# Attention, soft experts and MLP on one core: other spacing of converted weights, and products of zeros at the handover

## The chip, the cores and the metric

One Trainium2 chip, one of its cores. The metric is the device time of one execution in microseconds. The core's engines are TensorE (PE; its weight loads are PEld), VectorE (DVE), ScalarE (ACT), GpSimd (POOL) and SyncE (SP), which here only issues DMAs. Each engine executes its own queue in order.

## The reference

Three layers follow each other. Inputs are random; w_in, w_out, s and b of the last layer are 64-bit floats.

```python
def _attn_ref(q, k, v, cap):                       # (4, 12, 448, 64)
    scores = np.matmul(q, k.transpose(0, 1, 3, 2)) / np.sqrt(64)
    scores = cap * np.tanh(scores / cap)
    attn = np.exp(scores - np.max(scores, axis=-1, keepdims=True))
    attn = attn / (np.sum(attn, axis=-1, keepdims=True) + 1e-09)
    return np.matmul(attn, v)
def _moe_ref(x, phi, w1, w2):                      # x (1792, 768), 8 experts of 4 slots
    logits = x @ phi
    d = softmax(logits, axis=0); c = softmax(logits, axis=1)
    slot_input = (d.T @ x).reshape(8, 4, 768)
    for e in range(8):
        slot_out[e] = np.maximum(slot_input[e] @ w1[e], 0.0) @ w2[e]
    return c @ slot_out.reshape(32, 768)
def _moe2_ref(x, w_in, w_out, s, b):               # w_in (768, 2048), w_out (2048, 768)
    r = np.maximum(x @ w_in, 0.0)
    return (s * (r * r) + b) @ w_out
```

## The kernel before

The work has three stages on one core.

**Attention** (to about 257 us). For each of 24 pairs of heads, n, TensorE makes scores (`emit_qk`, L498, and `emit_qkl`, L515), ScalarE takes tanh and exp (L521, L535), VectorE and GpSimd add the exponentials (`emit_es`, `emit_esl`, L543, L549), and TensorE multiplies by v (`emit_av`, L556, `emit_avl`, L564). Copies out of PSUM (`copy`, L421 on ScalarE, L423 on VectorE) go to either engine. After every six pairs a softmax over tokens is carried on (`emit_smax`, `emit_sexp`, `emit_softt`, `emit_pn` at L716, `emit_slot` at L723, `emit_acc`).

Between this work the first weights of the MLP are turned from 64-bit floats to 32-bit ones. One block i is 128 rows of words: even i are blocks of w_in, odd i of w_out. A conversion is a load of 768 KB (`cv_load`, L208), two VectorE passes (`conv_a`, L221 and L224), one ScalarE pass (`conv_f`, L231), a sum on VectorE or GpSimd (`conv_m`, L234) and a store of 384 KB to a scratch tensor in DRAM (`cv_store`, L342), from which the MLP reloads it (`load_w`, L1117). 2*XS = 20 blocks of 32 are converted so; the others are loaded and converted during the MLP. Expert weights are loaded too (`load_next`, L364 for w1, L370 for w2): 14 blocks in rings that are open from the start, and six more of w2 in a ring that takes over the conversion's buffers (`cv_end`), so they come after the last store.

The order on each engine comes from `ListSchedule`: every operation has engines with planned costs, needs, a priority, buffers that it takes and frees, a latency that is added to its end (`lat`) and an earliest planned time (`after`). A candidate with a third number (the handicaps `HACT`, `DES`, `DESL`) is chosen as if it ended that much later. CV0 and CVP give a conversion's priority, CVA and CVT its load's earliest planned time, WA that of expert loads. Planned times set the order alone; at run time each engine waits for what it needs.

**Experts** (267 to 342 us). For each expert e, `emit_w1` (L1008) multiplies the slots by three blocks of w1, `emit_w1_t` transposes and takes the maximum with 0, `emit_w2` (L1029) multiplies by four blocks of w2 into `so`. The products of e+1 with w1 are issued ahead of those of e with w2. As blocks are used up their rings are reloaded. Further blocks lie in the room that attention's pools leave: two of w1, three of w2 (pools `px`) and four of w2 in `woe`.

**MLP** (to the end). `emit_sot` (L1278) transposes `so`. Since the first product of the MLP is linear in the slots, w_in is applied to these: for each of 16 blocks f, `emit_ma` (L1160) multiplies block and slots, `emit_ms` (L1168, ScalarE) copies the sum, `emit_mb` (L1173) repeats it over partitions, `emit_mc` (L1181, ScalarE) casts it, `emit_ml` (L1184, VectorE) keeps its rounding error. Then for each step x (512 tokens, one f; 16 values of f, then the next tokens): `emit_h` (L1191), the activation in four ScalarE passes (L1208, L1215 and twice L1221) to gh, its rounding error gl on VectorE (`emit_gl`, L1236), and `emit_y`, for each 128 tokens six products (L1254, L1255) with the high and low part of w_out. Those parts are made by `emit_hi` (a cast, L1146 on ScalarE, L1148 on VectorE, which it may use for f < FD = 3) and `emit_lo` (L1151, GpSimd). A second `ListSchedule` orders this stage. It plans `sot` at a time given by `after`, and everything that needs the slots behind that.

Of the kernel before, what the change touches and what calls it, by code (L numbers as in the profile page):

```python
# [10 lines left out]
F32 = mybir.dt.float32  # L11
# [91 lines left out]
def kernel(  # L103
# [87 lines left out]
    NE1 = KDM * FC  # L191
    XS = 10 if wide else 0
    scr_p = ctx.enter_context(tc.tile_pool(name="scr", bufs=1, space=bass.MemoryType.DRAM))
# [99 lines left out]
    def run(safe):  # L293
        W1N, W2N = (4, (4,)) if safe else (10, (4, 6))
        NV, NEB, NES, NXU, NXQ, NQK = 2, 5, 2, 4, 3, 2
        PX, PA, DES, DESL, HACT = -0.32, 2.0, 1.0, 0.5, 0.5
        CV0, CVP, CVA, CVT, WA = 9.33, 2.0, 20.19, 9.5, 30.39
        LATE = 0.6
# [593 lines left out]
        for bb in range(B):  # L892
            g = NQUAD * (bb + 1) - 1
            pr = 4 * g + 4 + PSO
            prev = [("ssum", bb - 1)] if bb else []
            op(("soft", bb), [(PE, 0.38)], emit_soft, [("lgr", g)], pr, [("tp", ("soft", bb))], [("lw", g)])
            op(("smax", bb), [(DVE, 0.66)], emit_smax, [("soft", bb)] + prev, pr, [("nm", bb)])
            op(
                ("sexp", bb), [(ACT, 0.8)], emit_sexp, [("smax", bb)], pr, [("pt", bb), ("al", bb)],
                [("tp", ("soft", bb))],  # L900
            )
            op(("ssum", bb), [(DVE, 0.2)], emit_ssum, [("sexp", bb)] + [("pn", bb)] * (bb == B - 1), pr + 1, [], [("nm", bb), ("al", bb)])
            op(("softt", bb), [(PE, 0.33)], emit_softt, [("sexp", bb)], pr, [("tp", ("softt", bb))], [("pt", bb)])
            op(("pn", bb), [(DVE, 0.2)], emit_pn, [("softt", bb)], pr, [("pn", bb)], [("tp", ("softt", bb))])

        need = []
        for i in range(len(cvs)):
            pr = CV0 + CVP * i
            op(("cl", i), [(SP, 2.19)], cv_load, [], pr - 6, [("w", i)], lat=3.0, after=CVA + CVT * i)
            op(("ca", i), [(DVE, 1.55)], cv_a, [("cl", i)], pr, [("cm", i), ("ce", i)], [("w", i)], port=BOTH)  # L910
# [13 lines left out]
        for i in range(n):  # L924
            sch.add(
                ("W", i), [(SP, 2.91 if i < W1N else 2.19)], lambda e: load_next(),
                prev + [("cend",)] * (i >= first), 1e3 + i, after=WA,
            )
            prev = [("W", i)]
# [44 lines left out]
        while can_load():  # L974
            load_next()


        h1m = h_p.tile([128, 2, 8, NS], F32, name="h1m")
# [46 lines left out]
        def emit_w2(e):  # L1025
            for fb in range(8):
                wt = w2t[e, fb // 2]
                for j in range(4):
# [3 lines left out]
                        start=(e == 0 and fb == 0), stop=(e == NE - 1 and fb == 7),  # L1032
                    )


# [119 lines left out]
        def emit_ma(f, _):  # L1155
            w = raw.pop(2 * f).rearrange("p (k f) -> p k f", k=KDM)
            ps = gtile()
            for i in range(2):
                for j in range(3):
# [3 lines left out]
                    )  # L1163
            msb[f] = ps

        def emit_ms(f, _):
# [4 lines left out]
        def emit_mb(f, _):  # L1171
# [4 lines left out]
            )  # L1176
            msb[f] = ps

        def emit_mc(f, _):
# [8 lines left out]
        def emit_h(x, _):  # L1188
            t0, n, f = steps[x]
            ps = gtile()[:, 0:n]  # L1190
            nc.tensor.matmul(out=ps, lhsT=mst[f], rhs=cs[:, t0:t0 + n], start=True, stop=True)  # L1191
            t = g_p.tile([128, n], F32, tag="r", name="r", bufs=NG)
            gh = g_p.tile([128, n], F32R, tag="gh", name="gh", bufs=NG)
# [48 lines left out]
        def emit_y(x, t, _):  # L1242
# [3 lines left out]
            i0 = t % per  # L1246
            if f == 0 and i0 == 0:
                yt[t // per] = pools3["y"].tile([128, 3, 512], F32, tag="y", name="y")
# [28 lines left out]
        def emit_sot(_):  # L1277
            nc.vector.transpose(out=sot.rearrange("p k c -> p (k c)"), in_=so)  # L1278
            px.close()
            pools3["wo"] = p2.enter_context(tc.tile_pool(name="wo", bufs=1, reuse_waits="tile"))  # L1280
            pools3["y"] = p2.enter_context(tc.tile_pool(name="ps_y", bufs=2, space=PSUM, reuse_waits="tile"))


# [6 lines left out]

        sch.add("sot", [(DVE, 0.3)], call(emit_sot), after=3.2)
        for i in range(NI):
# [110 lines left out]
```

## Time and profile before

| | |
|---|---|
| time, median of 3 runs | 627.92 us (627.23 to 629.49) |
| profiled execution | 627.3 us, of which the span from first to last instruction is 625.5 us |
| mean granted TensorE clock | 0.964 of full speed |
| TensorE busy | 574.5 us, 92% of the span |
| ScalarE, VectorE, GpSimd busy | 388.9, 374.5, 141.9 us |
| DMA | 139.25 MB, mean 223 GB/s |

All times within the profile count from the start of the span. In a row of an engine in order of time, the idle time ahead of the instruction stands in brackets with what ended it. TensorE's f32 products leave two records each, so that a block of w2 in `emit_w2`, eight products with each of two halves' quarters, shows as x16.

### The profile page before, as it was taken

What the parts mean: (1) busy time and instruction counts of PE and PEld (TensorE: products, weight loads), DVE (VectorE), ACT (ScalarE), POOL (GpSimd) and SP (SyncE); (2) the same over time, 40 slices, a digit from 0 to 9 for tenths busy, and PEclk for the clock granted to TensorE, in tenths of its full rate; (3) what the DMA queues carried; (4) which work ended last, traced back from release to release, by engine and by line L of the source; (5) the groups of instructions that cost most, each with busy time, mean ns of one, the idle gap of its engine ahead of it and who ended that gap; (6) DMA issues with size and microseconds to landing.
All of it is one profiled execution on the core that took longest, in us unless ns stands there. A gap on an engine that the chain in (4) does not pass through costs nothing.

```text
span 625.5 us, 10133 instructions
## 1 busy us (share of the span) xinstructions
PE 574.5 (92%) x3982; PEld 356.5 (57%) x3982; DVE 374.5 (60%) x543; ACT 388.9 (62%) x550; POOL 141.9 (23%) x84
## 2 busy tenths in 40 slices
PE   6999897999999999799656899999999999999895
PEld 3333232334333433356323688888888888888784
DVE  2586566969999778635400599952676688511211
ACT  3977676778876987200000788886756566665783
POOL 0163264343854425100000824220000000000000
PEclk9999998999999999879977799999999999999998
DMA  8579999995576534999999985500988779000201
GB/s 152 137 236 296 323 287 326 306 269 154 163 240 175 166 97 146 409 418 415 416 418 410 361 298 178 183 2 28 352 276 257 246 254 353 2 2 1 101 1 56
DMA packets 103175, 139.25 MB, mean 223 GB/s; under 512 B 52432, under 2 KB 84944, under 8 KB 100048
## 3 DMA queue, kind: packets, MB, share of 16 engines
q1 hardware_dynamic: 102176, 138.43, 66.5%
q8 instruction: 33, 0.54, 0.3%
q10 hardware_dynamic: 944, 0.10, 0.1%
q14 instruction: 22, 0.18, 0.1%
HBM read 125.14 MB, written 13.37 MB: 221 GB/s over the span
## 4 chain that ended last, share of the span: by engine, by line
PE 61%; DMA 22%; DVE 10%; ACT 3%; issue 2%; SPq 1%; ACTq 0%; DVEq 0%
PE y L1254 25%; PE y L1255 12%; DMA w2c<-in_moe_w_dram 9%; PE sp L498 6%; PE av L556 5%; DMA w<-in_moe_w_in_dram 3%; PE tr L455 3%; DMA w<-scr 2%; DMA vn<-in_v_dram 2%; DMA w<-in_moe_w_out_dram 2%; DVE cm L224 2%; PE gp L1191 2%; DMA woe<-in_moe_w_dram 2%; DVE es L549 1%; PE av L564 1%
## 5 line engine op out<-in xcount | busy, mean ns | idle before, releaser
L1254 PE MATMUL y<-wo,gh 128*128 128x512 f32 x336 | 127.0, 400 | 0.0
L521 ACT ACTIVATE e<-sp,tsc 128x896 f32<-128x896 f32 x84 | 83.3, 1006 | 40.7 <-PE sp L498 28.0
L1236 DVE TENSOR_TENSOR gl<-r,gh 128x512 fp32r<-128x512 f32 (+1 forms) x65 | 42.6, 657 | 99.6 <-ACT r L1221 99.5
L1255 PE MATMUL y<-wo,gh 128*128 128x256 f32 x336 | 94.4, 281 | 0.0
L535 ACT ACTIVATE e<-e,capt 128x896 f32<-128x896 f32 x84 | 84.9, 1040 | 0.4
L498 PE MATMUL sp<-qs,ks 64*128 64x448 f32 x288 | 75.8, 606 | 0.0
L1254 PEld LDWEIGHTS y<-wo,gh 128*128 128x128 f32 x336 | 63.2, 188 | 13.8 <-issue 1.6
L1208 ACT ACTIVATE r<-gp 128x512 f32<-128x512 f32 (+1 forms) x65 | 34.9, 539 | 58.1 <-PE gp L1191 56.4
L556 PE MATMUL av<-e,vn 128*64 128x448 f32 x288 | 69.1, 562 | 1.8 <-DMA vn<-in_v_dram 1.8
L1254 PE MATMUL y<-wo,gl 128*128 128x512 f32 x168 | 66.6, 397 | 0.0
L1255 PEld LDWEIGHTS y<-wo,gh 128*128 128x128 f32 x336 | 63.2, 188 | 1.7
L275 DVE TENSOR_REDUCE rng<-w 128x1 f32<-128x768 f32 x64 | 56.9, 945 | 0.9 <-DMA w<-in_moe_w_in_dram 0.9
L543 POOL TENSOR_TENSOR es<-e 128x896 f32<-128x896 f32 x17 | 38.0, 2233 | 57.3 <-ACT e L535 28.1
L1221 ACT ACTIVATE r<-r,bt,st 128x512 f32<-128x512 f32 (+1 forms) x65 | 49.1, 757 | 1.8
L1221 ACT ACTIVATE gh<-r,bt,st 128x512 fp32r<-128x512 f32 (+1 forms) x65 | 49.1, 757 | 1.6
L1254 PE MATMUL y<-woe,gh 128*128 128x512 f32 x112 | 44.2, 416 | 3.2 <-ACT ob L1272 2.0
L1255 PE MATMUL y<-wo,gl 128*128 128x256 f32 x168 | 47.1, 281 | 0.0
L224 DVE SCALAR_TENSOR_TENSOR cm<-w,cm 128x768 int32<-128x768 int32 x32 | 45.8, 1430 | 1.1
L1146 ACT CAST woe<-w 128x768 fp32r<-128x768 f32 x2 | 1.7, 830 | 71.2 <-DMA w<-scr 71.2
L498 PEld LDWEIGHTS sp<-qs,ks 64*128 64x128 f32 x288 | 23.4, 193 | 35.6 <-issue 12.3
L543 POOL TENSOR_TENSOR es<-es,e 128x896 f32<-128x896 f32 x14 | 32.7, 2337 | 37.7 <-DVE es L543 20.8
L549 POOL TENSOR_TENSOR es<-es,e 64x448 f32<-64x448 f32 x23 | 30.8, 1340 | 42.3 <-DVE es L543 21.7
(153 smaller groups left out, 947.4 us busy)
## 6 DMA issues: line engine op xcount, KB each, us to landing
w<-in_moe_w_in_dram SPq DMA_DIRECT2D x32, 768.0 KB, 5.9
w<-in_moe_w_out_dram SPq DMA_DIRECT2D x32, 768.0 KB, 6.0
w1c<-in_moe_w_dram SPq DMA_DIRECT2D x24, 1024.0 KB, 13.1
w2c<-in_moe_w_dram SPq DMA_DIRECT2D x26, 768.0 KB, 16.5
scr<-cm SPq DMA_DIRECT2D x20, 384.0 KB, 4.4
w<-scr SPq DMA_DIRECT2D x20, 384.0 KB, 5.7
qn<-in_q_dram SPq DMA_DIRECT2D x24, 224.0 KB, 4.2
kn<-in_k_dram SPq DMA_DIRECT2D x24, 192.0 KB, 4.5
```

What stands on the lines that cost most here:

```text
L224: nc.vector.scalar_tensor_tensor(out=m, in0=hi, scalar=-0x40000000, in1=m, op0=ALU.bitwise_and, op1=ALU.bitwise_or)
L275: nc.vector.tensor_reduce(out=rng[:, j, i:i + 1], in_=hi, axis=AX.X, op=o, apply_absolute_value=True)
L498: nc.tensor.matmul(out=sp[:, h, 0:S], lhsT=ks[n][rows, 128 * j:128 * j + 128], rhs=qs[n][rows, :], start=True, stop=True,)
L521: nc.scalar.activation(out=e, in_=spt.pop((n, j))[:, :, 0:S], func=AF.Tanh, scale=tsc)
L535: nc.scalar.activation(out=e, in_=e, func=AF.Exp, scale=capt)
L543: eng.tensor_tensor(out=t, in0=et[n, 0] if j == 1 else t, in1=et[n, j], op=ALU.add)
L549: eng.tensor_tensor(out=t, in0=t, in1=et["l", n // 2][r:r + KL, n % 2], op=ALU.add)
L556: nc.tensor.matmul(out=avt[n][64 * h:64 * h + 64, 0:S], lhsT=vt[n][:, KC * h + j, :], rhs=et[n, j][:, h], start=(j == 0 and n % 2 == 0), s ...
L1221: nc.scalar.activation(out=out, in_=in_, func=AF.Identity, scale=st, bias=bt)
L1236: eng.tensor_tensor(out=gl, in0=t, in1=f32(gh), op=ALU.subtract)
L1254: nc.tensor.matmul(out=ya, lhsT=lhsT, rhs=w[:, 0:512], start=first, stop=last)
L1255: nc.tensor.matmul(out=yb, lhsT=lhsT, rhs=w[:, 512:768], start=first and i0 == 0, stop=last and i0 == per - 1)
```

## The change

- XS is 9: blocks 18 and 19 (both halves of f = 9) are no longer converted in attention but in the MLP, so their scratch stores and reloads fall away.
- The planner's numbers for attention: conversions' loads are planned 8.5 apart (9.5 before) with priorities 1.85 apart (2.0), and are taken to land 6.0 after their issue (3.0); the first 14 expert loads are planned at least 5.0 apart; the handicap of ScalarE for copies is 0.2 (0.5); `pn` of the first three batches has a planned latency of 1.2 (0.6).
- `keep_busy`: products of a 128x128 bf16 tile of zeros with itself. In `emit_w2` of the last two experts ten stand behind each w2 block, four behind the last one; in the MLP three behind the first `emit_ma`, three behind the first `emit_mb` and eight behind the first `emit_h`, into the PSUM tile that the first `emit_y` overwrites, which is now allocated in `emit_sot`.
- `sot` is planned at 2.0 (3.2) in the MLP's schedule, which puts other operations ahead of the casts.

```diff
@@ tile_attention_moe_mlp_kernel
-    XS = 10 if wide else 0
+    XS = 9 if wide else 0
@@ run
-        PX, PA, DES, DESL, HACT = -0.32, 2.0, 1.0, 0.5, 0.5
-        CV0, CVP, CVA, CVT, WA = 9.33, 2.0, 20.19, 9.5, 30.39
+        PX, PA, DES, DESL, HACT = -0.32, 2.0, 1.0, 0.5, 0.2
+        CV0, CVP, CVA, CVT, WA, WT = 9.33, 1.85, 20.19, 8.5, 30.39, 5.0
...
-            op(("pn", bb), [(DVE, 0.2)], emit_pn, [("softt", bb)], pr, [("pn", bb)], [("tp", ("softt", bb))])
+            op(("pn", bb), [(DVE, 0.2)], emit_pn, [("softt", bb)], pr, [("pn", bb)], [("tp", ("softt", bb))], lat=LATE if bb == B - 1 else 1.2)
...
-            op(("cl", i), [(SP, 2.19)], cv_load, [], pr - 6, [("w", i)], lat=3.0, after=CVA + CVT * i)
+            op(("cl", i), [(SP, 2.19)], cv_load, [], pr - 6, [("w", i)], lat=6.0, after=CVA + CVT * i)
...
-                prev + [("cend",)] * (i >= first), 1e3 + i, after=WA,
+                prev + [("cend",)] * (i >= first), 1e3 + i, after=WA + WT * min(i, first - 1),
...
+        idle = h_p.tile([128, 128], BF16, name="idle")
+        nc.vector.memset(idle, 0.0)
+
+        def keep_busy(ps, n):
+            for _ in range(n):
+                nc.tensor.matmul(out=ps, lhsT=idle, rhs=idle, start=True, stop=True)
@@ emit_w2
+                if fb % 2 and e >= NE - 2:
+                    keep_busy(px_t("idle")[:, 0:128], 10 if e < NE - 1 or fb < 7 else 4)
@@ emit_ma, emit_mb
+            if f == 0:
+                keep_busy(yt[0][:, 0, 0:128], 3)
@@ emit_h
+            if x == 0:
+                keep_busy(yt[0][:, 0, 0:128], 8)
@@ emit_y
-            if f == 0 and i0 == 0:
+            if f == 0 and i0 == 0 and (x or t):
@@ emit_sot
+            yt[0] = pools3["y"].tile([128, 3, 512], F32, tag="y", name="y")
@@ run
-        sch.add("sot", [(DVE, 0.3)], call(emit_sot), after=3.2)
+        sch.add("sot", [(DVE, 0.3)], call(emit_sot), after=2.0)
```

How the order moves, at two places. First SyncE's queue at the end of attention, before; scr is the scratch store, vn the loads of v, w2c and w1c expert blocks:

```order
L441 DMA vn<-in_v_dram 128x2x192
L446 DMA vn<-in_v_dram 64x64 x2
L208 DMA w_2258<-in_moe_w_out_dram 128x1536
L342 DMA scr_115<-cm 128x768
L342 DMA scr_116<-cm 128x768
L441 DMA vn<-in_v_dram 128x2x192
L446 DMA vn<-in_v_dram 64x64 x2
L342 DMA scr_117<-cm 128x768
L370 DMA w2c<-in_moe_w_dram 128x1536 x6
L364 DMA w1c<-in_moe_w_dram 128x2048 x2
```

And now:

```order
L441 DMA vn<-in_v_dram 128x2x192
L446 DMA vn<-in_v_dram 64x64 x2
L342 DMA scr_115<-cm 128x768
L370 DMA w2c<-in_moe_w_dram 128x1536 x3
L441 DMA vn<-in_v_dram 128x2x192
L446 DMA vn<-in_v_dram 64x64 x2
L370 DMA w2c<-in_moe_w_dram 128x1536 x3
L441 DMA vn<-in_v_dram 128x2x192
L446 DMA vn<-in_v_dram 64x64 x2
L364 DMA w1c<-in_moe_w_dram 128x2048 x2
```

The last of 18 stores stands ahead of the last two loads of v, and the six w2 blocks stand among these; before, the last of 20 stores and all six stood behind the last load of v.

Second, ScalarE's first operations of the MLP, before (ms is the copy of a sum, mste the cast of it, woe the cast of w_out, r and gh the activation):

```order
L1146 CAST woe<-w_3233 128x768
L1168 COPY ms<-gp 96x128 x2
L1181 CAST mste<-gp 128x128 x2
L1208 ACTIVATE r<-gp 128x256 x2
L1215 ACTIVATE r<-r 128x256 x2
```

And now:

```order
L1180 COPY ms<-gp 96x128
L1195 CAST mste<-gp 128x128
L1180 COPY ms<-gp 96x128
L1224 ACTIVATE r<-gp 128x256 x2
L1195 CAST mste<-gp 128x128
L1231 ACTIVATE r<-r 128x256 x2
```

The cast of w_out of f = 0 is gone from the head of ScalarE's queue; it is on VectorE now, behind `sot` and ahead of the first `emit_ml`, and the chain of f = 0 runs ahead of that of f = 1.

## Rows read from the trace of the kernel before

**Rows 1.** The page's chain that ended last, by engine.

```profile
PE 61%; DMA 22%; DVE 10%; ACT 3%; issue 2%; SPq 1%; ACTq 0%; DVEq 0%
```

**Rows 2.** Busy time by stretch: us, engines' busy us (instructions), clock, DMA share, GB/s.

```profile
100.00:200.00 100.00, 97.10 (x566) 36.75 (x564) 87.18 (x117) 75.47 (x88) 51.34 (x27) 0.99 0.76 229
243.00:246.00 3.00, 2.67 (x14) 0.54 (x14) 2.77 (x5) 2.05 (x3) 2.34 (x2) 1.00 0.00 0
325.00:330.00 5.00, 4.30 (x43) 1.76 (x46) 0.36 (x1) 0.00 (x0) 0.00 (x0) 0.50 1.01 416
349.00:352.00 3.00, 2.73 (x9) 2.03 (x10) 1.24 (x2) 3.00 (x7) 1.72 (x2) 0.50 1.00 372
390.00:400.00 10.00, 10.00 (x76) 8.16 (x74) 9.59 (x13) 8.27 (x16) 2.81 (x2) 1.00 0.61 198
```

**Rows 3.** SyncE's issues in order of time, end of attention: start, us.

```profile
247.63 0.33 SPq L342 DMA_DIRECT2D scr<-cm  x1
248.00 4.68 SPq L370 DMA_DIRECT2D w2c<-in_moe_w_dram  x6
252.73 1.24 SPq L364 DMA_DIRECT2D w1c<-in_moe_w_dram  x2
...
271.72 6.42 SPq L364 DMA_DIRECT2D w1c<-in_moe_w_dram  x6
```

**Rows 4.** The page's DMA issues: count, KB each, median us to landing.

```profile
w<-in_moe_w_in_dram SPq DMA_DIRECT2D x32, 768.0 KB, 5.9
...
w1c<-in_moe_w_dram SPq DMA_DIRECT2D x24, 1024.0 KB, 13.1
w2c<-in_moe_w_dram SPq DMA_DIRECT2D x26, 768.0 KB, 16.5
```

**Rows 5.** TensorE in order of time, attention: three rows that begin with a wait.

```profile
70.11 0.97 PE L556 MATMUL av<-e,vn 128*64 128x448 f32 x4 [1.75 <-DMA vn<-in_v_dram]
...
97.46 0.64 PE L723 MATMUL sl<-xq,pn 112*32 112x256 f32 x8 [3.68 <-DVE pn L716]
...
144.09 0.75 PE L455 MATMUL tr<-ident,kn 128*128 128x128 f32 x4 [0.72 <-DVE dn L423]
```

**Rows 6.** Waits of VectorE to 267 us: total, times, longest.

```profile
DVE cm L221 <- DMA w<-in_moe_w_in_dram: 8.4, 4, 2.9
```

**Rows 7.** TensorE in order of time, last expert blocks and start of the MLP.

```profile
329.35 2.92 PE L1029 MATMUL so<-w2c,h1m 128*32 128x192 f32 x48
...
335.26 0.86 PE L1029 MATMUL so<-w2c,h1m 128*32 128x192 f32 x16 [1.12 <-DMA w2c<-in_moe_w_dram]
...
340.83 1.51 PE L1029 MATMUL so<-woe,h1m 128*32 128x192 f32 x16 [0.39 <-DMA woe<-in_moe_w_dram]
...
346.40 0.50 PE L1191 MATMUL gp<-cs,mste 128*128 128x512 f32 x1 [0.85 <-DVE mste L1184]
...
350.67 0.79 PE L1254 MATMUL y<-woe,gl 128*128 128x512 f32 x1 [0.27 <-DVE gl L1236]
...
354.82 0.50 PE L1254 MATMUL y<-woe,gh 128*128 128x512 f32 x1
```

**Rows 8.** ScalarE, then VectorE, in order of time, start of the MLP.

```profile
342.85 0.83 ACT L1146 CAST woe<-w 128x768 fp32r<-128x768 f32 x1 [71.16 <-DMA w<-scr]
343.98 0.26 ACT L1168 COPY ms<-gp 96x128 f32<-96x128 f32 x1 [0.30 <-DMA w<-scr]
...
344.76 1.27 DVE L1148 CAST woe<-w 128x768 fp32r<-128x768 f32 x1 [1.96 <-DMA w<-scr]
346.05 0.50 DVE L1184 TENSOR_TENSOR mste<-gp,mste 64x128 fp32r<-64x128 f32 x2
```

**Rows 9.** MLP conversions: L224 (ns min/median/max), last weights' correction, their use.

```profile
L224 DVE SCALAR_TENSOR_TENSOR cm<-w,cm x12: 958/960/2541, 360.6 to 409.1; 128x768 int32<-128x768 int32 x12
...
417.01 0.29 DVE L1184 TENSOR_TENSOR mst<-gp,mst 64x128 fp32r<-64x128 f32 x1 [2.38 <-ACT mst L1181]
...
424.14 0.40 PE L1191 MATMUL gp<-cs,mst 128*128 128x512 f32 x1
```

More of the change, by code (lines that the diff above doesn't have):

```diff
@@ L1177, in emit_mb @@
             msb[f] = ps
+            if f == 0:
+                keep_busy(yt[0][:, 0, 0:128], 3)
         def emit_mc(f, _):
```

## The prediction

> **What bounds the kernel now.** I read the chain that ended last first, then busy time by stretch, then the order of the DMA issues, then each engine in order of time where one stage hands over to the next. The chain is 61% TensorE and 22% DMA [rows 1], and the stretches say where each of the two holds. Attention (0 to 257 us) is TensorE: 97.10 of 100 us busy in its middle [rows 2], so only its few waits can be won there. The experts (about 267 to 342 us) are DMA: 416 GB/s in 325 to 330 us, where TensorE works at a granted clock of 0.50, the lower of its two levels (1.2 of 2.4 GHz), without being late for anything but data [rows 2]. The MLP (from 355 us) is TensorE again, 10.00 of 10 us [rows 2]; it starts when the last expert block has come and been handed on [rows 7, 8]. So time can come from waits inside attention, from bytes that needn't pass in the expert stage, and from the handover.
>
> The sum is made against the profiled execution: 627.3 us, of which 625.5 are the span. The median of the three runs shown is 627.92, 0.6 above it.
>
> **1. Expert loads that move into attention.** Here is most of the gain. The second ring of six w2 blocks takes the room of the conversion's buffers, so its loads stand behind the last conversion's store. That store is issued at 247.63 and the six at 248.00 [rows 3], while DMA moved 0 GB/s just before, from 243 to 246 us [rows 2]. From there the engines don't rest until the last block is used at 340.83 [rows 7]. Bytes in that stretch: 14 w1 blocks of 1024 KB and 28 of w2 of 768 KB [rows 4] (so many stand in the queue behind that point), 36.7 MB; at 417 GB/s that is 88.0 us, and 340.83 - 248.00 = 92.8, so 4.8 us are start and end.
> The change has 18 conversions, not 20, and spaces their loads by 8.5, not 9.5. In the new order the last store stands before the last two loads of v, three of the six loads behind it, three more ahead of the last v. They move 4.7 MB (11.3 us) while the queue is half idle.
> They don't give back 11.3. What comes next are two w1 blocks that lie in attention's own buffers, issued at 252.73 with no wait shown [rows 3], so free at that time at the latest. From there 32.0 MB remain: 76.7 us, and with the same 4.8 the last block is there at 334.2. A second limit is the ring of w1: its first reload is at 271.72 [rows 3], when TensorE has read its first block, and 24.4 MB follow it: 58.6 + 4.8 gives 335.1. Against 340.83 that is 6.6 and 5.7; I take **-6.2**. Bounds: -11.3 (all room already free at 248) and 0 (the last store as late as now).
> The two blocks that are not converted any more cost no bytes in this stage, since their loads come in the MLP.
>
> **2. Attention itself.** Removed: two conversions, each three VectorE steps and one of ScalarE. Three copies go from VectorE to ScalarE (handicap 0.2 for 0.5), three sums from GpSimd to VectorE. TensorE's own work is the same, so the gain is bounded by its waits. The large ones are 1.75 us for a v load, 3.68 for VectorE's pn and 0.72 for a copy [rows 5]. The last two are VectorE standing in a conversion whose load is late: 8.4 us of waits for the w_in loads in all [rows 6]. The planner now counts 6.0 us for such a load and not 3.0, against a median of 5.9 [rows 4], so it will put the conversion behind other work. Of the 4.4 us of these two waits I take **-2.5**. Bounds: -6.2 (all three go) and +3.7 (the largest comes back elsewhere: every engine's order is new, and the conversions are closer together). The spacing of the first 14 expert loads by 5 us changes little: in the queue they stand among the same heads as before.
>
> **3. The handover.** At the end of the experts a block comes every 1.9 us (335.26 and 340.83 are three apart); its 16 pieces take 0.86 us at the full clock and 1.51 at the lower [rows 7].
> First the order. Now ScalarE's cast of the first w_out block waits until 342.85 for its reload and stands ahead of the copy of the first sum (343.98); VectorE's cast, 344.76 to 346.03, stands ahead of the correction of the first weights (346.05) [rows 8]; the first h starts at 346.40 [rows 7]. In the change ScalarE copies the sum first and VectorE does the first cast. From the last block's arrival, in durations of rows 7 and 8: products 0.86, transpose and hand-over 0.55, sums of one block 0.5, copy 0.4, broadcast 0.4, cast 0.4; but VectorE's cast can't start before 2.0 (342.85 - 340.83) and takes 1.27, so the correction ends at 3.6 and h starts there, not at 5.57: -1.9.
> Then the clock. From 349 to 352 us it is 0.50 [rows 2]. From the first product of gl (350.67) to the step at 354.82, with which the full clock is back, pass 4.15 us of products with hardly a wait [rows 7]; at twice the clock the same ones take half, 2.05: -2.1. That holds if the products of zeros keep the clock up.
> What is late next: the second block's gl. ScalarE still has two casts and three passes ahead of it, which lets TensorE wait about half a microsecond: +0.5. Together **-3.5**; bounds -5 and -1.2 (the clock stays down).
> **The zeros' own price** has no row before. A tile product of 16 pieces takes 0.86 us, 0.054 each [rows 7]; a transposition of 128x128 in f32, four in 0.75, takes 0.19 [rows 5]. The work is a dense series of small products into one bank, nearest to the former, so I take 0.06. From 329.35 to 341.69 lie eight blocks [rows 7], 12.3 us; in the change they hold 8 x 0.86 + 74 zeros x 0.06 = 11.3, so the zeros fit in the waits for data: 0. They stop fitting at (1.9 - 0.86) / 10 = 0.104 each; at 0.19 they and the products take 21.0 us, 8.7 more.
> The Trainium skill (TensorE: Matmul & The Clock Gate, Back-to-back issue gap) gives about 81 ns for a sustained product of 128 columns with its weight load; by that, as an estimate, a block takes 0.86 + 0.81 = 1.67 of its 1.9 us and the term is 0 too. No run here shows it.
>
> **4. Two more conversions in the MLP.** VectorE is at 9.59 of 10 us in 390 to 400 [rows 2], and 14 blocks instead of 12 are converted there. Each costs VectorE three passes over the same 768 columns; the middle one takes 0.96 us at the median and 2.54 at most [rows 9], and with that for the other two a block is 2.9 to 4.5 us, two of them 6 to 9. The last weights are corrected at 417.01 and used at 424.14 [rows 9], 7.1 us of cover; in the new order that correction stands behind gl of step 14 instead of 12. I take **+0.5**; bounds 0 and +6.6 (none of it covered). A wait here would be TensorE's, for h of steps 13 to 15.
>
> Everything behind 430 us is the same work in the same order: 0.
>
> **Sum**: 627.3 - 6.2 - 2.5 - 3.5 + 0.5 = **615.6 us**.
>
> **The rivals.**
> (a) Attention loses what it could win: the denser conversions meet expert loads, a v or k load lands late, and a wait like the one of 3.68 us comes again. For it: 70.11 is such a wait for v [rows 5]. Against it: the planner allows for late loads now. 615.6 + 2.5 + 3.7 = 621.8.
> (b) The clock falls in spite of the zeros: 615.6 + 2.3 = 617.9. For it: at 325 us TensorE was 4.30 of 5 us busy and still at 0.50 [rows 2].
> (c) VectorE can't finish 14 conversions in time: TensorE waits for the last weights, 615.6 + 6.1 = 621.7. For it: 9.59 of 10. Against it: 7.1 us of cover. The second step's spread, 958 to 2541 ns [rows 9], is what decides. By the Trainium skill (SBUF — State Buffer, SBUF: two separate sides) VectorE and GpSimd share one port pair under an exclusive lock and the loser waits out the other's whole instruction; the trace agrees as far as the spread goes, and if all 14 lost it, as an estimate 14 x 1.6 us would use up the cover and bring this case.
> (d) The change doesn't do what it says: the last store comes no earlier in time, and the six loads still start at 248: 621.8.
> (e) The other side: the zeros run one after the other, each waiting for the one before it, since they write the same bank. Then one costs what a lone small product costs; if that is 0.27 us or more, the last eight blocks take 8 x 0.86 + 74 x 0.27 = 26.9 us in place of 12.3, 14.6 late: 615.6 + 14.6 = 630.2, slower than before. It begins to hurt at 0.104 and decides at about 0.23. Against it: the 16 pieces of a block also go to one bank, and take 0.054 each [rows 7].
>
> **How the numbers follow.** Forecast 0.64; (a) 0.16; (b) 0.08; (c) 0.06; (d) 0.03; (e) 0.03. A measurement of this kernel can tell about 0.5%, 3.1 us, from no change: faster is under 624.8, slower over 631. All cases but (e) end faster; (a) and (c) together would reach 628, and losses in attention beyond its bound are possible, so faster 0.89, same 0.08, slower 0.03. The range takes (a) to (d) on the high side with 1.7 more for losses that come together, 623.5; on the low side the bound of attention's gain (-3.7) and the rest of the DMA and handover bounds added in quadrature (5.1 and 1.5): 6.5, so 609 and, rounded outward, 608.5.
>
> **What would show it.** Right: the six w2 loads issued between about 220 and 240 us; DMA busy at 230 to 246; the last expert block used about 9 us earlier (334.6, less what attention gives); granted clock 1.00 from then to the first y; h about 3.6 us behind that block; the VectorE waits for conversion loads mostly gone; no TensorE wait between 400 and 430. Wrong: the zeros over 0.1 us apart; TensorE waits for v over 4 us; DMA idle between 255 and 275 us, which would eat the first term; the clock at 0.5 behind the last block.

## The result, and the profile after

The change takes 617.45 us (median of 4 runs, 616.00 to 618.41) beside 627.58 for the kernel before on the same chip: ratio 0.9831, 95% interval 0.9802 to 0.986, so it is faster by 1.7%, and the interval lies clear of 1. The prediction was 615.6 us, with a range of 608.5 to 623.5. The profiled execution has a span of 615.5 us, 10.0 less than before.

Busy time by stretch of the kernel after, with the columns of [rows 2]: engines' busy us and instructions, granted clock, DMA share, GB/s.

```profile
100.00:200.00 100.00, 97.06 (x566) 35.98 (x564) 80.98 (x114) 76.72 (x90) 43.16 (x25) 0.98 0.78 229
243.00:246.00 3.00, 3.00 (x18) 1.29 (x18) 2.11 (x4) 2.94 (x4) 0.00 (x0) 1.00 0.05 16
325.00:330.00 5.00, 5.00 (x88) 3.41 (x88) 0.00 (x0) 0.00 (x0) 0.00 (x0) 1.00 1.01 415
349.00:352.00 3.00, 3.00 (x20) 2.64 (x18) 0.84 (x2) 2.41 (x6) 2.31 (x2) 1.00 0.99 370
390.00:400.00 10.00, 10.00 (x67) 8.46 (x67) 9.83 (x11) 9.12 (x16) 3.15 (x2) 1.00 0.50 165
```

Attention's middle is as full of TensorE as before (97.06 of 100 us). Around the end of the experts the granted clock is 1.00 where it was 0.50, at the same 415 GB/s. DMA still rests at 243 to 246 us, though its work begins earlier; the next rows say why.

SyncE's issues at the end of attention, as in [rows 3]: start, duration.

```profile
217.38 0.33 SPq L342 DMA_DIRECT2D scr<-cm  x1
217.76 3.10 SPq L370 DMA_DIRECT2D w2c<-in_moe_w_dram  x3
...
229.63 1.53 SPq L370 DMA_DIRECT2D w2c<-in_moe_w_dram  x3
...
238.71 8.60 SPq L364 DMA_DIRECT2D w1c<-in_moe_w_dram  x2
...
270.32 6.11 SPq L364 DMA_DIRECT2D w1c<-in_moe_w_dram  x6
```

The last store is issued 30 us earlier, and the six w2 blocks, three at 217.76 and three at 229.63, 30 and 18 us earlier than at 248.00. They have landed by 243 us (share 0.05 above), and the two w1 blocks behind them take 8.60 us to issue, because the second waits for TensorE to leave its buffer. So the limit is the first reload of the w1 ring, at 270.32.

TensorE in order of time, as in [rows 7]: the late v load, the last block with zeros ahead of it, the first h, the first product of gl.

```profile
88.44 1.76 PE L556 MATMUL av<-e,vn 128*64 128x448 f32 x4 [2.52 <-DMA vn<-in_v_dram]
...
268.32 1.93 PE L1016 MATMUL h1p<-w1c,slt 128*32 128x256 f32 x16 [0.51 <-DVE slt L1007]
...
332.85 0.73 PE L984 MATMUL idle<-idle 128*128 128x128 bf16 x10
333.96 0.86 PE L1037 MATMUL so<-woe,h1m 128*32 128x192 f32 x16 [0.38 <-DMA woe<-in_moe_w_dram]
...
337.59 0.50 PE L1205 MATMUL gp<-cs,mste 128*128 128x512 f32 x1
...
341.75 0.50 PE L1270 MATMUL y<-woe,gl 128*128 128x512 f32 x1 [0.47 <-DVE gl L1252]
```

From such rows of the two kernels the 10.0 us of span split into three. The first expert product lies at 268.32 (269.73 before): 1.41 less. From it to the last block pass 65.64 us (71.10): 5.46 less. From the last block to the end of the span pass 281.54 (284.67): 3.13 less. The last piece holds h at 3.63 us behind the block (5.57) and gl's first product at 7.79 (9.84).

ScalarE, then VectorE, at the start of the MLP, as in [rows 8].

```profile
336.02 0.26 ACT L1180 COPY ms<-gp 96x128 f32<-96x128 f32 x1 [65.73 <-PE gp L1170]
...
335.90 0.56 DVE L1158 CAST woe<-w 128x768 fp32r<-128x768 f32 x1 [0.63 <-DMA w<-scr]
337.16 0.29 DVE L1198 TENSOR_TENSOR mste<-gp,mste 64x128 fp32r<-64x128 f32 x1 [0.70 <-ACT mste L1195]
```

ScalarE begins with the copy of the sum. VectorE's cast takes 0.56 us (1.27 before) and ends at 336.46; the correction then waits 0.70 us for ScalarE's cast of the weights. So here the chain of sum, copy, broadcast and cast sets the time of h, and not VectorE's cast.

The end of the conversions, as in [rows 9]: all 14 of L224, the last weights' correction, and the product that uses it.

```profile
L224 DVE SCALAR_TENSOR_TENSOR cm<-w,cm x14: 957/959/2653, 351.8 to 407.5; 128x768 int32<-128x768 int32 x14
...
414.83 0.29 DVE L1198 TENSOR_TENSOR mst<-gp,mst 64x128 fp32r<-64x128 f32 x1
...
415.18 0.50 PE L1205 MATMUL gp<-cs,mst 128*128 128x512 f32 x1
```

The correction ends at 415.12 and the product starts at 415.18: of 7.1 us of cover nearly none is left, and TensorE waited 0.2 us at most.

### The profile page after: what moved, and what is told of

Read it like the earlier page. It is cut to its first block, busy times and chain, and to the rows that moved or that the text cites. A ratio compares the mean times of both kernels' runs of the same rounds, so it can differ in the third digit from the quotient of the medians.

```text
span 615.5 us, 10293 instructions
## 1 busy us (share of the span) xinstructions
PE 577.1 (94%) x4070; PEld 357.2 (58%) x4070; DVE 370.5 (60%) x545; ACT 390.1 (63%) x552; POOL 133.5 (22%) x81
## 4 chain that ended last, share of the span: by engine, by line
PE 74%; DMA 12%; DVE 7%; ACT 3%; POOL 2%; issue 1%; SPq 0%; POOLq 0%; DVEq 0%; ACTq 0%
PE y L1270 24%; PE y L1271 12%; PE sp L498 9%; PE av L556 8%; DMA w2c<-in_moe_w_dram 6%; DMA w<-scr 4%; PE tr L455 4%; PE h1p L1016 2%; PE gp L1205 2%; PE rowt L599 2%; PE dn L586 2%; PE lg L614 2%; PE sp L515 2%; DMA vn<-in_v_dram 2%; PE xt L646 1%; PE av L564 1%
## 5 line engine op out<-in xcount | busy, mean ns | idle before, releaser
L1252 DVE TENSOR_TENSOR gl<-r,gh 128x512 fp32r<-128x512 f32 (+1 forms) x65 | 47.6, 732 | 91.4 <-ACT r L1237 91.1
L556 PE MATMUL av<-e,vn 128*64 128x448 f32 x288 | 70.5, 570 | 2.5 <-DMA vn<-in_v_dram 2.5
L1180 ACT COPY ms<-gp 96x128 f32<-96x128 f32 x16 | 4.1, 256 | 67.5 <-PE gp L1170 67.0
L224 DVE SCALAR_TENSOR_TENSOR cm<-w,cm 128x768 int32<-128x768 int32 x32 | 43.0, 1343 | 1.1
L543 POOL TENSOR_TENSOR es<-e 128x896 f32<-128x896 f32 x13 | 28.3, 2174 | 57.2 <-ACT e L535 37.6
L1231 ACT ACTIVATE r<-r 128x512 f32<-128x512 f32 (+1 forms) x65 | 37.2, 575 | 1.8
```

The lines of the kernel that those rows point to most:

```text
L224: nc.vector.scalar_tensor_tensor(out=m, in0=hi, scalar=-0x40000000, in1=m, op0=ALU.bitwise_and, op1=ALU.bitwise_or)
L543: eng.tensor_tensor(out=t, in0=et[n, 0] if j == 1 else t, in1=et[n, j], op=ALU.add)
L556: nc.tensor.matmul(out=avt[n][64 * h:64 * h + 64, 0:S], lhsT=vt[n][:, KC * h + j, :], rhs=et[n, j][:, h], start=(j == 0 and n % 2 == 0), s ...
L1231: nc.scalar.activation(out=t, in_=t, func=AF.Square)
L1252: eng.tensor_tensor(out=gl, in0=t, in1=f32(gh), op=ALU.subtract)
```

## The experiments

All times are medians, ratios are to the kernel before, measured on the same chip with the run. From each profile three lengths are read as above: the first expert product (F), from it to the last w2 block (B), from that block to the end of the span (M). For before they are 269.73, 71.10 and 284.67, for the change 268.32, 65.64 and 281.54.

**The change again.** No edit.

> The change itself once more, as the yardstick for the runs beside it on the same chip. All theories: ratio to before 0.983 (0.980 to 0.986), some 10.3 us less. In the profile the block-to-first-gl stretch should again be 7.8 us and the last w2 block 65.6 us behind the first expert product; the first product itself may lie anywhere between 265 and 269 us, since the four profiles with this attention order that exist so far differ by 4 us there.

616.88 us, ratio 0.986 (0.9821 to 0.9898). F 266.05, B 66.00, M 282.15. B and M repeat within 0.6 us here. F doesn't: over the ten profiles with these numbers of attention it runs from 264.90 to 271.05, mean 267.5, while the order of before gives 269.73 and, in the run of the handover alone, 267.52. A gain of 1.4 us in attention can't be told from this scatter. Much of the scatter is a wait and the clock behind it: in the profile with 264.90 TensorE waits 1.48 us at 88 us, and the granted clock is 1.00 from 80 to 100 and from 160 to 180 us; in the one with 271.05 it waits 3.97 us at 90 us, and the clock is 0.83 and 0.91 in these stretches.

M hides a second scatter of this kind. In every run TensorE waits 2.0 us for a ScalarE copy out of PSUM (ob), some 43 us before the end. Here is the product behind that wait, in the kernel before, in the change, and in the second run without zeros below:

```profile
583.56 0.50 PE L1254 MATMUL y<-woe,gh 128*128 128x512 f32 x1 [2.00 <-ACT ob L1272]
```

```profile
573.65 0.50 PE L1270 MATMUL y<-woe,gh 128*128 128x512 f32 x1 [2.01 <-ACT ob L1288]
```

```profile
574.14 0.60 PE L1270 MATMUL y<-woe,gh 128*128 128x512 f32 x1 [2.00 <-ACT ob L1288]
```

In 7 of the 14 profiles, the third among them, the clock falls behind this wait, and the rest of the span takes 43.3 to 43.8 us; in the other 7 it takes 41.9 to 42.2. So the handover is read below from a fourth length, T, from the last w2 block to the product behind this wait. It is 242.73 for before, 239.69 for the change and 240.05 in this repetition.

**The six early loads, held back.** A first try and a second. A small store to DRAM, of a column of attention's last step but one, was put ahead of the six, which wait for its issue:

```diff
+    late = scr_p.tile([128, 1], F32, name="late")
...
+        sch.add(
+            "hold", [(SP, 0.1)], lambda e: nc.sync.dma_start(out=late, in_=xut[NP - 2][:, 0:1]),
+            [("avc", NP - 2), ("ld", "v", NP - 1), ("cend",)], 1e3,
+        )
...
-                prev + [("cend",)] * (i >= first), 1e3 + i, after=WA + WT * min(i, first - 1),
+                prev + ["hold"] * (i >= first), 1e3 + i, after=WA + WT * min(i, first - 1),
```

> The change, with its six second-ring w2 loads held back by a small store that reads the copy of av of the last pair but one (249.0 us in the changed kernel); all else as there. Theory (the gain of 6 us between the first expert product and the last block is bytes that passed earlier): the six are issued near 249.7, 36.7 MB at 417 GB/s plus 4.8 us follow, the last block is used at about 342, 8 us later than in the changed kernel, and the time is about 625.5. Rival 1 (the first w1 reload at 270.3 sets the end, and the queue has room before it): last block at most 2 us later, time under 619.5. Rival 2 (the gain came from fewer bytes or from attention): no difference.

634.55 us, ratio 1.0138 (1.0082 to 1.0194): far more than either theory gave. F 266.55, B 80.95, M 283.5. The windows of this run around the store, which was issued at 247.86, and behind it:

```profile
245.00:250.00 5.00, 4.67 (x31) 1.63 (x31) 4.67 (x6) 2.05 (x2) 1.55 (x1) 1.00 0.93 20
250.00:255.00 5.00, 4.32 (x26) 1.58 (x19) 0.38 (x2) 1.60 (x3) 0.00 (x0) 1.00 0.39 26
255.00:260.00 5.00, 1.94 (x15) 1.24 (x13) 4.51 (x8) 0.00 (x0) 0.45 (x1) 1.00 0.61 170
```

The DMA engines move 20 and 26 GB/s. (Their busy share doesn't tell more: the 0.93 comes from a single microsecond, 249 to 250, that is booked at 4.55.) The store, 4 bytes from each of 128 partitions, took 7.9 us to land, and the expert loads behind it in the queue moved at most 46 GB/s from 250 to 258 us. The run measures its own store, so a second one reads a single partition:

```diff
-            "hold", [(SP, 0.1)], lambda e: nc.sync.dma_start(out=late, in_=xut[NP - 2][:, 0:1]),
+            "hold", [(SP, 0.1)], lambda e: nc.sync.dma_start(out=late[0:1, :], in_=xut[NP - 2][0:1, 0:1]),
```

> The change with its six second-ring loads held back once more, this time behind a store of 4 bytes from one partition: the first try held them behind a store of 4 bytes from each of 128 partitions, and the DMA engines then moved 20 to 26 GB/s from 245 to 255 us, so its 634.6 us is that store's doing. Theory A, the six loads' early start is what brings the last block near: the six start at 248 us as before, first product to last block 71 us as before instead of 65.6, time 622 to 624, ratio 0.992 to 0.994. Rival, the block's time follows the first reload behind the first product alone: 65.6 us and 617.5, ratio 0.983.

626.32 us, ratio 0.9988 (0.9961 to 1.0015). F 268.94, B 72.99, M 283.57. SyncE's issue of the six, the window after it, and the last block (lines are five lower here):

```profile
250.61 3.07 SPq L371 DMA_DIRECT2D w2c<-in_moe_w_dram  x6
```

```profile
255.00:260.00 5.00, 3.28 (x18) 1.84 (x18) 2.70 (x5) 0.87 (x2) 0.00 (x0) 1.00 1.01 422
```

```profile
341.93 0.86 PE L1042 MATMUL so<-woe,h1m 128*32 128x192 f32 x16 [0.38 <-DMA woe<-in_moe_w_dram]
```

The last block comes 91.3 us after the issue of the six; before it was 92.8. So the expert stage is that much DMA work from the moment the six may start. They start 2.6 us later than before here, which is why B is above 71. With the rest of the change left in, holding them costs 7 us in B and 8.0 in the time by the ratios (0.9988 against 0.986; 9.4 by the medians). Of the 7 us, 5.1 undo what the change won in B, and 1.9 are the hold's own delay. The rival, that the block follows the first product alone, is out. The hold also keeps back the two w1 loads behind the six, as the order of before does.

**The handover alone.** All attention numbers as before (XS, HACT, the spacings, pn's latency, and the lead of the conversion loads; two of them shown); zeros and the transpose at 2.0 kept.

```diff
-    XS = 9 if wide else 0
+    XS = 10 if wide else 0
...
-            op(("cl", i), [(SP, 2.19)], cv_load, [], pr - 6, [("w", i)], lat=6.0, after=CVA + CVT * i)
+            op(("cl", i), [(SP, 2.19)], cv_load, [], pr - 6, [("w", i)], lat=3.0, after=CVA + CVT * i)
```

> The handover part of the change (zeros, ScalarE's sums ahead of its casts, the transpose of the sums placed at 2.0) with ten conversions in attention and all attention numbers as before. Theory A, the three parts add up: first expert product and last block as before (269.7 and 340.8 in the profile, within the spread of 4 us), last block to the end 3.6 us shorter than before (no conversion more in the MLP): ratio 0.994 to 0.995. Rival, the parts are not independent (the handover's gain needs the earlier ring or hides only where DMA is early): ratio 0.998 to 1.000.

623.54 us, ratio 0.9958 (0.9933 to 0.9982): nearer to theory A (0.994 to 0.995) than to its rival. F 267.52, B 70.31, M 282.87, T 239.50; h 3.65 us behind the block. M is 1.8 us shorter than before and not 3.6 as expected; T, which leaves out the clock's fall near the end, is 3.2 shorter.

**Attention alone.** No zeros, transpose at 3.2.

```diff
-            for _ in range(n):
+            for _ in range(0):
...
-        sch.add("sot", [(DVE, 0.3)], call(emit_sot), after=2.0)
+        sch.add("sot", [(DVE, 0.3)], call(emit_sot), after=3.2)
```

> The change without zeros and with the slots planned at 3.2 again: only the planner's numbers for attention and the nine pairs of blocks remain. Theory (the parts add up; behind the last block the change wins 3.1 us, up to it 6.9): 617.45 + 3.1 = 620.6, handover from last block to first gl product about 9.8 us as before. Rival (the parts lean on each other): 623 or more, or under 619.

619.83 us, ratio 0.9902 (0.9869 to 0.9935). F 266.68, B 65.39, M 284.73, T 242.83: B as in the change, M and T as before, h 5.64 behind the block. The two halves' gains, 0.0042 and 0.0098, add up to 0.0140; the change's two measurements are 0.0169 and 0.014. Within intervals of some 0.003 each the two halves add up. The numbers within the attention half were not taken apart, but for the loads' lead and the number of blocks below.

**No zeros, twice.** Only the loop's count, as above.

> The change without the products of zeros (the tile of zeros stays). Theory (zeros keep TensorE's clock up through the handover, 1.00 from 325 us on): the granted clock falls to about 0.5 to 0.6 between the last blocks and the first steps of the MLP, the last block's 16 pieces take 1.5 and not 0.86 us, the first gl product comes about 1 us later after the block and the steps behind it another 1 us: plus 1.5 to 2.5 us, 619 to 620. Rival (the order on ScalarE alone made the handover shorter, the first gl waits for ScalarE whatever the clock is): plus 0 to 0.5.

615.93 us, ratio 0.9841 (0.9807 to 0.9874), below the 619 to 620 expected; F 268.90, B 64.21, M 283.89, T 242.02. The last block's 16 pieces still took 0.86 us and not 1.5, since the clock fell only behind them; h came 4.07 and gl's first product 9.58 us behind the block (3.63 and 7.79 in the change).

> The change without its products of zeros, a second time beside the change on one chip, because the first run of it (ratio 0.9841) left the zeros' worth inside the noise. Theory A, the clock is worth what the profile showed (2.35 us from the last block to the end: 281.5 with zeros, 283.9 without): ratio 0.004 above the change's of this batch, some 2.3 us. Theory B, the time does not feel it (another wait in the MLP takes what the clock gives): the same ratio within 0.001. Either way the granted clock should read 0.50 between the last block and the first products of the MLP without zeros, 1.00 with them.

618.56 us, ratio 0.9864 (0.9828 to 0.99), beside the change's 616.88 on that chip; F 266.74, B 64.79, M 286.17, T 242.61; h 4.72 and gl's first product 9.66 behind the block.

**Zeros in the handover alone.**

```diff
-                    keep_busy(px_t("idle")[:, 0:128], 10 if e < NE - 1 or fb < 7 else 4)
+                    keep_busy(px_t("idle")[:, 0:128], 0)
```

> The change with the zeros between the last experts' products left out and the 14 zeros of the handover (behind the first three products of the MLP) kept. Theory A, the handover's own zeros hold the clock: granted clock 1.00 from the last w2 block to 345 us, last block to first gl product 7.8 us, and the zeros between the experts do nothing. Rival B, the clock falls in the waits for the last blocks, before the handover's zeros come, and is not back in time: 0.50 from some 333 to 345 us, 9.6 us from block to first gl, 2.3 to 3.9 us from block to end above the change's, as in the two runs without any zeros. The time by A as the change (ratio 0.983 to 0.986), by B 0.984 to 0.990; the profile decides, for in the time the two lie within each other's intervals.

617.72 us, ratio 0.9868 (0.9826 to 0.991). F 271.05, B 64.77, M 284.18, T 242.15. Windows of the change's second run, of the second run without zeros, and of this one, in this order:

```profile
325.00:333.00 8.00, 6.53 (x119) 4.16 (x108) 0.03 (x1) 0.00 (x0) 0.00 (x0) 1.00 1.02 403
333.00:337.00 4.00, 3.61 (x47) 2.37 (x45) 2.16 (x4) 1.49 (x6) 1.83 (x1) 1.00 1.01 389
337.00:345.00 8.00, 6.98 (x52) 5.04 (x53) 4.95 (x7) 7.85 (x18) 7.36 (x4) 1.00 0.94 317
```

```profile
325.00:333.00 8.00, 3.63 (x64) 1.75 (x64) 0.36 (x1) 0.00 (x0) 0.00 (x0) 0.94 1.02 408
333.00:337.00 4.00, 3.55 (x28) 2.25 (x29) 1.44 (x4) 0.79 (x3) 2.15 (x2) 0.50 1.03 398
337.00:345.00 8.00, 7.38 (x39) 5.23 (x40) 2.70 (x5) 6.99 (x16) 6.45 (x4) 0.50 0.98 358
```

```profile
325.00:333.00 8.00, 4.30 (x77) 2.12 (x72) 0.05 (x1) 0.00 (x0) 0.00 (x0) 0.86 1.02 415
333.00:337.00 4.00, 3.23 (x40) 1.18 (x32) 0.00 (x0) 0.00 (x0) 0.00 (x0) 0.50 1.02 402
337.00:345.00 8.00, 7.46 (x62) 4.55 (x57) 2.65 (x6) 2.88 (x10) 3.84 (x3) 0.53 1.02 386
```

Without zeros between the last experts TensorE is busy 3.63 and 4.30 of 8 us there, and the clock then stands at 0.50; with them it is busy 6.53 and the clock stays at 1.00. The handover's own 14 zeros come too late to keep it: rival B holds for the clock. It is back by 344.5 us, 8.7 us behind the block, but by then h is late: it comes 5.51 and gl's first product 11.19 us behind the block, later than without any zeros (B had expected 9.6). Some of that is the last block itself, whose pieces took 1.51 us here, and some the zeros ahead of h, which ran at the lower clock too; how much each is was not measured.

The price of the lower clock is seen in T: 242.0, 242.6 and 242.2 without the experts' zeros, 239.5 to 240.3 in the six profiles with all zeros and this order (the change's two, the two with held loads, the handover alone, and the one with the short load lead below): 2.4 us on the mean. (M would give 2.9 from the change's two profiles, but 0.5 of it is the clock's fall near the end, which came in one of the three runs without these zeros and in neither of those two.)

B however is shorter without: 64.2, 64.8, 64.8 and, in the run of attention alone, 65.4, against 65.6, 66.0 and three more of 65.6 to 65.7 below, 0.9 us on the mean. Of this, 0.8 is there before the first zero runs: the last two expert loads are issued 46.5 us behind the first product on the mean without zeros (45.9 to 47.3) and 47.3 with them (46.6 to 47.9), over 6 us ahead of the first zeros. So it isn't shown to be their doing.

The one pair on the same chip differs by 1.7 us in the time (616.88 against 618.56), but the intervals overlap, and the first run without zeros has the lowest median of all: no run shows the zeros' worth in the time beyond its noise.

**Three times the zeros between the experts.**

```diff
-                    keep_busy(px_t("idle")[:, 0:128], 10 if e < NE - 1 or fb < 7 else 4)
+                    keep_busy(px_t("idle")[:, 0:128], 30 if e < NE - 1 or fb < 7 else 4)
```

> The change with 30 zeros instead of 10 behind each second w2 block of the last two experts. A zero costs 0.066 us (10 in 0.66 us), so a pair with its zeros takes TensorE 1.3 us more and the room of the waits (at 10 zeros the last blocks still wait 0.4 to 1.0 us for their loads) is used up. If zeros are on the path from then on: the last block some 5 to 9 us later than in the change, time 622 to 626. Rival, the loads are later still than TensorE with 30 zeros: last block 64 us behind the first product as in the change, time 616 to 618.

622.93 us, ratio 0.9941 (0.9905 to 0.9977). F 267.24, B 71.20, M 283.5. TensorE in order of time in this run:

```profile
333.30 0.86 PE L1037 MATMUL so<-w2c,h1m 128*32 128x192 f32 x16
334.09 1.85 PE L984 MATMUL idle<-idle 128*128 128x128 bf16 x30
335.87 0.86 PE L1037 MATMUL so<-woe,h1m 128*32 128x192 f32 x16
```

The last blocks don't wait for data any more. From the first zero to the next block 1.78 us pass: 0.059 a zero. B is 5.2 to 5.6 us longer than in the change's two runs, the lower end of what was expected if the zeros are on the path.

**The transpose late, zeros kept.** The second edit of the attention run without its first.

> The change with the slots planned at 3.2 instead of 2.0, zeros kept: ScalarE's first operation of the MLP is again the cast of the first w_out block. Theory (that cast stands ahead of the first sum's copy and waits for its reload): h starts about 1 to 2 us later behind the last block than in the changed kernel, plus 1 to 2 us, 618.5 to 619.5. Rival (the clock alone made the handover shorter): plus 0 to 0.5.

619.02 us, ratio 0.9891 (0.9857 to 0.9926). F 264.90, B 65.65, M 290.05, T 246.48: h is 5.64 us behind the block as before and gl's first product 9.91, and then this, in order of time on VectorE, GpSimd and TensorE, and in the windows around it:

```profile
345.08 4.11 DVE L1252 TENSOR_TENSOR gl<-r,gh 128x512 fp32r<-128x512 f32 x1 [2.76 <-ACT r L1237]
```

```profile
343.19 5.45 POOL L1161 TENSOR_TENSOR wo<-w,wo 128x768 fp32r<-128x768 f32 x3
```

```profile
349.25 0.80 PE L1270 MATMUL y<-woe,gl 128*128 128x512 f32 x1 [2.88 <-DVE gl L1252]
```

```profile
345.00:349.00 4.00, 1.36 (x8) 0.92 (x7) 3.92 (x1) 2.86 (x6) 3.64 (x3) 0.95 1.01 390
349.00:355.00 6.00, 5.75 (x26) 4.32 (x27) 4.04 (x7) 2.03 (x4) 0.00 (x0) 0.50 0.87 323
```

A gl of 128x512 that takes 0.69 us at 347.68 of the first run without zeros took 4.11 and ended 0.55 us behind GpSimd's run of three. TensorE waited 2.88 us, and after 1.36 busy of 4 us the clock fell to 0.50 for the next 6. The profiled execution is the slowest of its six (622.43); the median is 2 us over the change's. The order by itself can't be told from the time: 0.9902 for the old one without zeros against 0.9841 and 0.9864 for the new one, 0.9891 with zeros against 0.9831 and 0.986, and the intervals of each pair overlap. T says more. Old order without zeros: 242.73 and 242.83. New order without: 242.02 and 242.61. Old order with zeros: 246.48, in one profile and with this collision. Both: 239.5 to 240.3. So each half alone gave 0.1 to 0.8 us or a loss, and the two together 3.0: the earlier copy pays off only when the products behind it run at the full clock.

**Eight blocks in attention instead of nine.**

```diff
-    XS = 9 if wide else 0
+    XS = 8 if wide else 0
```

> The change with eight blocks converted in attention instead of nine, two more conversions in the MLP (16). Theory A, the change is at the edge there: its 14th conversion is ready 0.1 us before the product that needs it, VectorE starts one about every 4.6 us, so two more are some 9 us late, less what attention gives back (1.4 us in the change): 623 to 626. Rival, VectorE draws them forward into its idle time and only 1 to 3 us are lost or none: 615 to 619.

619.42 us, ratio 0.9868 (0.9807 to 0.993). F 268.33, B 65.56, M 284.4. All 16 conversions and the correction they end in:

```profile
L224 DVE SCALAR_TENSOR_TENSOR cm<-w,cm x16: 957/958/2507, 349.9 to 408.2; 128x768 int32<-128x768 int32 x16
...
417.19 0.29 DVE L1198 TENSOR_TENSOR mst<-gp,mst 64x128 fp32r<-64x128 f32 x1
```

The last conversion starts at 408.2 (407.5 with 14), so theory A with its 9 us is out: VectorE did draw them forward. The change isn't at an edge there, as the 0.06 us of cover seemed to say. M is 2.2 to 2.9 us longer, but 1.9 of that is again the clock's fall near the end; T is 240.66, with one new TensorE wait of 0.81 us for a copy out at 429.67. F gave nothing back.

**Conversion loads planned 3 us ahead, as before.**

```diff
-            op(("cl", i), [(SP, 2.19)], cv_load, [], pr - 6, [("w", i)], lat=6.0, after=CVA + CVT * i)
+            op(("cl", i), [(SP, 2.19)], cv_load, [], pr - 6, [("w", i)], lat=3.0, after=CVA + CVT * i)
```

> The change with the loads of the blocks to convert due 3 us ahead of their use as before, instead of 6. Theory A, the earlier loads are what shortened attention: VectorE's waits for them (8.4 us before) come back and the first expert product lies 1 to 3 us later than in the change, ratio 0.987 to 0.991. Rival, nine conversions at wider spacing need no earlier load: the same ratio as the change, or better by up to the 2.5 us that TensorE now waits for a v load at 88 us, which stands behind those loads: 0.980 to 0.985.

626.64 us, ratio 1.0017 (0.9984 to 1.0049): the direction of theory A at several times its size. F 278.52, B 65.65, M 282.93, T 239.64. Waits of VectorE up to 270 us (total, times, longest) and TensorE's largest wait in this stretch:

```profile
DVE cm L221 <- DMA w<-in_moe_w_out_dram: 7.5, 2, 4.0
...
DVE cm L221 <- DMA w<-in_moe_w_in_dram: 4.9, 3, 2.8
```

```profile
189.51 1.20 PE L455 MATMUL tr<-ident,kn 128*128 128x128 f32 x4 [3.73 <-DVE dn L423]
```

```profile
100.00:200.00 100.00, 91.37 (x520) 34.33 (x521) 74.39 (x104) 70.02 (x84) 50.23 (x28) 0.95 0.75 217
```

VectorE stands 12.4 us for late conversion loads, none of which the change's two profiles have, and TensorE, which stands behind it, is busy 91.37 of 100 us in attention's middle. With the rest of the change's numbers the longer lead is needed; together they leave F about where it was, and let the last store and the first of the six loads come 30 us earlier. That the closer spacing is what makes the longer lead needed is likely but not shown: the handicap, pn's latency and the expert loads' spacing changed too, and no run changes one of them alone.

## Why the prediction was right

**1. Expert loads into attention (-6.2 predicted).** -5.46 in B, and the held loads show the cause. Of the two limits the second held. The last block lies 63.64 us behind the first w1 reload (270.32 to 333.96); the prediction's 58.6 + 4.8 was 63.4. Its sign of trouble, idle DMA between 255 and 275 us, appeared in small (share 0.75 from 270 to 275), since the six were through and nothing else might start; and DMA was busy to 243 us, not to 246 as foretold.

**2. Attention (-2.5).** -1.41 in the pair of profiles, less than the scatter of one order. VectorE's waits for conversion loads went, as said; the 3.68 us behind them went too; new ones came (2.52 for a v load at 88 us, 1.80 for a VectorE sum). The prediction's reason, that counting 6.0 us puts the conversions behind other work, is right, but it stood in the wrong place in the sum: no run shows that it is worth 2.5 us against before; what it does is prevent a loss of 10 us that the change's other numbers bring without it.

**3. Handover (-3.5).** M with the fourth term is -3.13 against -3.0, and T, over six profiles, is 3.0 shorter than the 242.8 of the old order without zeros. The sum is right; how it is made up is not. The prediction counts the order and the clock as two gains that add up, -1.9 and -2.1. The order alone gave 0.1 to 0.8 in T: without the zeros h comes 4.07 to 4.72 us behind the block, and gl's first product only 0.2 to 0.3 earlier than in the old order. The zeros without the order gave a loss in the one profile there is. Both gave 3.0, gl's first product 2.05 earlier. That h came 3.63 us behind the block against 3.6 worked out is in part luck: the 3.6 rested on a VectorE cast of 1.27 us that ends at 3.3, but the cast took 0.56, and the chain over ScalarE, worked out at 3.1 ahead of the correction, was what h waited for. The wait put at +0.5 for the second block's gl doesn't show; TensorE's 0.47 us stands at the first block's gl (0.27 before).

Zeros cost 0.06 each: 0.059 measured. By the Trainium skill (TensorE: Matmul & The Clock Gate, Back-to-back issue gap) it would have been 0.081; the trace gives less, and the term is 0 by either. Rival (e) is out. Why the last loads are issued up to 2 us later in some runs than in others, which moves B, stays open.

**4. Two more conversions (+0.5).** From 358 to 500 us TensorE waits nowhere more than 0.2 us, and the two longer waits behind that (0.8 and 2.0 us, for copies out) stand in before too: 0. Even 16 fit, for one wait of 0.81 us. Rival (c) rested on a busy share of 9.59 in 10, which says that VectorE had work to draw forward, not that it was late. What it feared does exist elsewhere: by the Trainium skill (SBUF — State Buffer, SBUF: two separate sides) VectorE waits out GpSimd's whole instruction. The 4.11 us of gl in the run with the late transpose agree in kind and go further: gl outlasted two of GpSimd's three instructions of 1.8 us.

In the profiled executions the forecast was 1.7 us too low: 1.1 of it is attention, 0.7 the first term, -0.1 the other two. The 1.1 is within attention's scatter, so that part of the agreement is neither earned nor refuted.

## What to carry to other kernels

When one stage is bound by DMA and the stage ahead leaves DMA idle, ask what each load waits for: here six loads waited for a store, and 30 us earlier for that store gave most of the gain, until the next thing, a buffer that TensorE must read first, became the limit. Changes act together: without the longer lead the rest of the change lost all that it won, and the new order of the handover paid off only with the clock kept up. A stretch may vary from run to run by more than the step under study (6 us in attention here), so read a step's gain from an interval between two marks inside the profile rather than from the end, and set the second mark ahead of the next wait behind which the clock may fall.

## What was not expected of the hardware

- A store of 4 bytes from each of 128 partitions took 7.9 us to land, and the large loads queued behind it moved at most 46 GB/s from 2 to 10 us behind its issue; with a single partition they moved 316 GB/s and more from 2 us behind it.
- VectorE's 0.69 us subtraction stretched to 4.11 beside a run of three GpSimd instructions. TensorE waited 2.88 us for it and then ran at its lower clock (1.2 of 2.4 GHz) for some 6 us: one collision cost more than the wait itself.
- Products of zeros in the handover alone brought the clock back only 8.7 us behind the last block, when h was already late (5.51 us behind it, 3.63 in the change); those ahead of it, between the waits for data, kept it.
- The same wait of 2.0 us near the end was followed by the lower clock in 7 of 14 profiles, which made the rest of the span 1.1 to 1.9 us longer.
